# Loading the k of units 4 to 8 with tokens on rows, maxima through memory, and reading channel weights in pairs

## The chip, the cores and the metric

The kernel runs on one core of a Trainium2 chip. The metric is the device time of one execution in microseconds (us); a kernel's time is the median of its runs. Five engines work side by side, each through its own instructions in order: TensorE (PE in the profile, its weight loads PEld), VectorE (DVE), ScalarE (ACT), GpSimd (POOL) and SyncE (SP). Here nearly all loads are issued by SP, so its queue is an order too: a load that has to wait for a buffer holds up every load behind it.

## The reference

Eight batches of eight heads, 576 tokens, head width 64. An attention without a token-by-token matrix is followed by a mixer over tokens and a mixer over channels:

```python
q_s = np.exp(q - np.max(q, axis=-1, keepdims=True))      # softmax of q over the head's 64 columns
q_s = q_s / (np.sum(q_s, axis=-1, keepdims=True) + 1e-09)
k_s = np.exp(k - np.max(k, axis=2, keepdims=True))       # softmax of k over the 576 tokens
k_s = k_s / (np.sum(k_s, axis=2, keepdims=True) + 1e-09)
x = einsum(q_s, einsum(k_s, v))                          # 64x64 per head, then (batch, 576, 512)
h = np.maximum(x.T @ w_tok1, 0.0) @ w_tok2               # tokens: 576 -> 256 -> 576
u = x + h.T
h2 = np.maximum(u @ w_ch1, 0.0) @ w_ch2                  # channels: 512 -> 1536 -> 512
out = u + h2
```

The four weight matrices come as float64, the rest as float32.

## The kernel before

**Units.** A unit is two heads of one batch; there are 32, numbered 0 to 31 here as in the code (n). A unit's tokens lie in five chunks of 128 (the last one is the 64 left-over tokens, laid out twice). Units 0 to 7 (`early`) go through `stage_qT`, `stage_kv`, `stage_y`, `stage_h1` and two `stage_u`: q is turned by TensorE (L349, L354), `kv` is the product of k and v (L319), `y` that of q and w_tok1 (L387), `h1` that of y and kv (L395), and `stage_u` adds q times kv (L440) and the token mixer's second product (`token_products`, L422) into one bank, which `empty` copies to `uh` and `ul`. Units 8 to 31 run later, between the products of the channel mixer.

**The softmax of k** (`softmax_k`) takes its maximum over tokens. Before, units 0 to 7 load only `kt`, the k with the 128 columns on rows: VectorE reduces each row (L249), ScalarE does the exponential (L253), TensorE turns the five chunks back (four at L256, one at L259), and ScalarE copies them out to `k_t` (L257, L260). Unit 8 loads `kt` and `k`: its maxima are spread onto a diagonal, multiplied with ones (L272) and copied to the tile `mb`; GpSimd then subtracts `mb` from `k_t` (L278) and ScalarE does the exponential (L279). Units 9 to 31 do the same, but the maxima get to `mb` through memory: VectorE transposes them in `dg` (L265), SP writes them to `row` in DRAM (L267) and reads that back to all 128 rows (L268). There is one `dg` and one `mb`.

**Weights.** Channel weights come in 24 pieces of 128x512 float64: for each f from 0 to 11 one of w_ch1 and one of w_ch2. `load_ch(f)` loads both. `narrow` makes float32 out of a piece in six steps on 128x512 elements, five on VectorE (L201, L203, L204, L206, L208) and one on ScalarE (L202), and `split` cuts it into a high part (ScalarE) and a low part (VectorE, L126). Pieces take turns in the tiles `stg` of two pools.

**Order.** A scheduler that simulates the program's time line sets the order of the instructions on each engine and in SP's queue. So an instruction that is put in somewhere, or a buffer that comes free at another time, moves others around it. `behind(x)` lets instructions be issued only after those in x. Buffers in the early pools are three deep (`NB`), those of `kt` two.

**Channel mixer.** `ch1` (L477) and `ch2` (L637) work on groups of 512 tokens; steps with f 0 to 3 of the first two groups come first, while later weights are still being narrowed.

Of the kernel before, what the change touches and what calls it, by code (L numbers as in the profile page):

```python
# [8 lines left out]
F32 = mybir.dt.float32  # L9
# [6 lines left out]
P = 128  # L16
# [4 lines left out]
def attn_mixer_kernel(ctx: ExitStack, tc: tile.TileContext, q, k, kt, v, wt, out, dims):  # L21
# [81 lines left out]
    for i in range(3):  # L103
        slots[i][1] = lay.tile([P, NJ, CW], F32R, name=f"ul{i}")
    mb = lay.tile([P, P], F32, name="mb")
    h2 = [[lay.tile([P, CW], F32R, name=f"h2h{i}"), None] for i in range(2)]
    kv_ring = [kv_tile(lay, 0)]
    for i in range(2):
        h2[i][1] = lay.tile([P, CW], F32R, name=f"h2l{i}")
    cw = {}  # L110

    def ch_rows(f0, f1):
        late = ctx.enter_context(tc.tile_pool(name=f"late{f0}", bufs=1))
        t = late.tile([P, f1 - f0, NJ, 4, P], F32R, name=f"cw{f0}")
# [24 lines left out]

    conv = [(stg, cv)]  # L140


    def load_unit(b, j):
        n = b * NJ + j
        u = {"b": b, "j": j, "n": n, "early": n < NE}
        if n >= PAIRED:
            return u
        pool = early if u["early"] else ld
        t = pool.tile([P, C1 * P], F32, name="kt_t", bufs=NB - 1 if u["early"] else 1)
        nc.sync.dma_start(t, kt[n])  # L150
        u["kt"] = t
        t = pool.tile([P, C1, P], F32, name="q_t")
        nc.sync.dma_start(t.rearrange("p c d -> p (c d)"), q[n])
        u["q"] = t
        t = pool.tile([P, C1, P], F32, name="k_t")
        if not u["early"]:
            nc.sync.dma_start(t.rearrange("p c d -> p (c d)"), k[n])
        u["k"] = t
        return u
# [35 lines left out]

    def narrow(raw, n, out):


        w0, w1 = raw[:, 0:n, 0], raw[:, 0:n, 1]
        s = conv[-1][1].tile([P, C1 * P], U32, name="cv_s")[:, 0:n]  # L200
        nc.vector.tensor_scalar(s, w1, 20, 0x7FF, op0=ALU.logical_shift_right, op1=ALU.bitwise_and)  # L201
        nc.scalar.activation(s, s, AF.Relu, bias=ebias, scale=2.0**23)  # L202
        nc.vector.scalar_tensor_tensor(s, w1, 0x80000000, s, op0=ALU.bitwise_and, op1=ALU.bitwise_or)  # L203
        nc.vector.tensor_scalar(w1, w1, 0xFFFFF, 0x100000, op0=ALU.bitwise_and, op1=ALU.bitwise_or)  # L204
        f1 = w1.bitcast(F32)
        nc.vector.scalar_tensor_tensor(f1, w0, 2.0**-32, w1, op0=ALU.mult, op1=ALU.add)  # L206
# [26 lines left out]

    def load_ch(f):
        for x, at in ((0, AT_C1), (2, AT_C2)):
            t = load_weights(at + f).rearrange("p (n m) -> p n m", n=NJ)
            narrowed[:] = [split(cw[f][x], cw[f][x + 1], t, nc.vector)]
# [7 lines left out]
    def softmax_k(u):  # L245
        ktt = u["kt"]
        through = u["n"] > NE
        mc = dg[:, 0:1] if through else sm.tile([P, 1], F32, name="mc")
        nc.vector.tensor_reduce(mc, ktt, axis=AX.X, op=ALU.max)  # L249
        kx = u["k"]  # L250
        if u["early"]:
            nc.vector.tensor_scalar(mc, mc, -1.0, None, op0=ALU.mult)
# [28 lines left out]
    def softmax_q(u):  # L281
# [18 lines left out]
        nc.vector.reciprocal(st[:, 2, :], st[:, 1, :])  # L300
        nc.vector.tensor_tensor(qt, qt, st[:, 2, :].unsqueeze(2).broadcast_to([P, G, D]), op=ALU.mult)
        if u["early"]:
# [439 lines left out]
    for n in range(NE):  # L742
        if n + 2 < NE:
            begin(n + 2)
            soft(n + 2)
        if n + 1 < NE:
            stages[n + 1][0]()
            stages[n + 1][1]()
        stages[n][2]()
        stages[n][3]()  # L750
        if n >= NE - F_HEAD:
            load_ch(n - (NE - F_HEAD))
        if n == NE - 1:
            with behind(emptied):
                split_tok1()
# [211 lines left out]
```

## Time and profile before

| | |
|---|---|
| median of 3 runs | 796.18 us (795.25 to 796.74) |
| the profiled execution | 796.4 us, of which its span is 794.5 us |
| mean granted TensorE clock over the span | 0.994 |
| PE busy | 779.0 us |
| DVE, ACT, POOL busy | 526.7, 326.5, 85.1 us |
| HBM read, written | 54.85 MB, 9.45 MB |

The span is what the profiler saw between the first and the last instruction; the rest of the execution's time lies around it. The shares of the page are means over stages with different limits: units 0 to 7 fill roughly the first 80 us, where VectorE and ScalarE are nearly as busy as TensorE; later TensorE works alone most of the time.

### The profile page before, as it was taken

To read this page: it belongs to the slowest core of one execution; us is meant where nothing else is said; L and a number is where in the kernel's file an instruction comes from. 1 tells how busy PE (TensorE), PEld (TensorE's weight loads), DVE (VectorE), ACT (ScalarE), POOL (GpSimd) and SP (SyncE) were. 2 spreads that over 40 slices of the span, in tenths; PEclk is the share of its full clock that TensorE was granted. 3 is DMA by queue.
4 is the path that set the end of the run, shared out by engine and by line. 5 is a ranking of instruction groups with operands and counts; after the bars stand their busy time and mean duration, and the time that the engine had idled before them with its cause. 6 is when DMAs were issued, how large, how long until landed. Compare 5 with 4: busy or idle time off the path is not lost.

```text
span 794.5 us, 12177 instructions
## 1 busy us (share of the span) xinstructions
PE 779.0 (98%) x4478; PEld 650.9 (82%) x4478; DVE 526.7 (66%) x1208; ACT 326.5 (41%) x824; POOL 85.1 (11%) x77
## 2 busy tenths in 40 slices
PE   6899999999999999999999999999999999999998
PEld 6688888887888888888888888888888888888886
DVE  6899998897777445755575455564668558975441
ACT  6876544435553343344433434333434413232100
POOL 1000010003122111120201101111111000000020
PEclk8899999999999999999999999999999999999999
DMA  9753422334334221513141212313240000000011
GB/s 289 249 175 104 143 91 101 112 89 133 83 92 137 66 72 37 152 37 100 38 120 54 81 57 74 111 38 85 51 125 18 1 1 28 26 1 0 1 67 40
DMA packets 64786, 65.08 MB, mean 82 GB/s; under 512 B 41944, under 2 KB 45272, under 8 KB 64728
## 3 DMA queue, kind: packets, MB, share of 16 engines
q1 hardware_dynamic: 60120, 56.06, 24.1%
q10 hardware_dynamic: 4608, 8.26, 2.8%
q8 instruction: 35, 0.57, 0.3%
q14 instruction: 23, 0.19, 0.1%
HBM read 54.85 MB, written 9.45 MB: 81 GB/s over the span
## 4 chain that ended last, share of the span: by engine, by line
PE 87%; DVE 6%; ACT 3%; DMA 2%; issue 1%; POOL 1%; DVEq 0%; POOLq 0%; ACTq 0%
PE ps_o L637 30%; PE ps_h L477 26%; PE ps_h L586 7%; PE ps_h L387 6%; PE ps_h L422 5%; PE ps_h L637 4%; PE ps_h L319 2%; PE ps_h L456 2%; PE ps_h L395 1%; ACT q_t L292 1%; DMA q_t<-in_q 1%; PE ps_o L422 1%; DVE stack L374 1%; PE ps_o L387 1%; DVE st L286 0%
## 5 line engine op out<-in xcount | busy, mean ns | idle before, releaser
L637 PE MATMUL ps_o<-h2h,cw 128*128 128x512 f32 x768 | 226.6, 391 | 0.0
L477 PE MATMUL ps_h<-uh,cw 128*128 128x512 f32 x672 | 210.4, 393 | 0.0
L637 PEld LDWEIGHTS ps_o<-h2h,cw 128*128 128x128 f32 x768 | 142.5, 188 | 29.8 <-issue 0.4
L481 DVE SCALAR_TENSOR_TENSOR h2l<-ps_h,h2h 128x512 fp32r<-128x512 f32 x84 | 57.8, 688 | 153.2 <-ACT h2h L480 152.6
L477 PEld LDWEIGHTS ps_h<-uh,cw 128*128 128x128 f32 x672 | 123.7, 188 | 24.4 <-issue 0.4
L637 PE MATMUL ps_o<-h2l,cw 128*128 128x512 f32 x384 | 137.4, 390 | 0.0
L477 PE MATMUL ps_h<-ul,cw 128*128 128x512 f32 x336 | 130.9, 390 | 0.0
L480 ACT ACTIVATE h2h<-ps_h 128x512 fp32r<-128x512 f32 x84 | 49.9, 594 | 90.5 <-PE ps_h L477 80.0
L126 POOL TENSOR_TENSOR ql<-q_t,qh 128x640 fp32r<-128x640 f32 x24 | 39.5, 1647 | 425.6 <-ACT qh L125 390.4
L637 PEld LDWEIGHTS ps_o<-h2l,cw 128*128 128x128 f32 x384 | 72.0, 188 | 15.1
L477 PEld LDWEIGHTS ps_h<-ul,cw 128*128 128x128 f32 x336 | 63.1, 188 | 13.4
L374 DVE COPY stack<-cv_s 32x128 f32<-32x128 f32 (+1 forms) x264 | 55.7, 229 | 3.5 <-PE ps_h L456 0.6
L278 POOL TENSOR_TENSOR k_t<-k_t,mb 128x640 f32<-128x640 f32 x24 | 37.9, 1579 | 109.8 <-DMA mb<-row 78.7
L279 ACT ACTIVATE k_t<-k_t 128x640 f32<-128x640 f32 x24 | 17.7, 739 | 66.2 <-POOL k_t L278 66.2
L495 DVE TENSOR_TENSOR ul<-ps_h,ul 128x512 f32<-128x512 f32 x40 | 27.3, 687 | 24.1 <-PE ps_h L586 23.7
L374 ACT COPY stack<-cv_s 32x160 f32<-32x160 f32 (+1 forms) x120 | 37.4, 311 | 2.8 <-DVE cv_s L364 1.5
L434 ACT CAST uh<-ps_h 128x288 fp32r<-128x288 f32 (+8 forms) x84 | 25.1, 317 | 27.2 <-PE ps_h L456 22.6
L297 ACT ACTIVATE q_t<-q_t 128x640 f32<-128x640 f32 x28 | 20.7, 740 | 32.0 <-DVE q_t L296 31.9
L422 PE MATMUL ps_h<-w2h,hh 128*128 128x288 f32 x112 | 33.7, 302 | 0.0
L422 PE MATMUL ps_h<-w2l,hh 128*128 128x288 f32 x112 | 33.3, 298 | 0.0
L637 PE MATMUL ps_h<-cw 128*128 128x512 f32 x144 | 33.0, 389 | 0.0
L422 PE MATMUL ps_h<-w2h,hl 128*128 128x288 f32 x112 | 32.6, 296 | 0.0
(250 smaller groups left out, 1277.0 us busy)
## 6 DMA issues: line engine op xcount, KB each, us to landing
stg<-in_w SPq DMA_DIRECT2D x28, 512.0 KB, 3.3
kt_t<-in_kt SPq DMA_DIRECT2D x32, 320.0 KB, 3.3
q_t<-in_q SPq DMA_DIRECT2D x32, 320.0 KB, 3.0
k_t<-in_k SPq DMA_DIRECT2D x24, 320.0 KB, 3.0
out<-stg ACTq DMA_DIRECT2D x27, 256.0 KB, 2.3
v_t<-in_v SPq DMA_DIRECT2D x46, 128.0 KB, 3.1
part<-in_v SPq DMA_DIRECT2D x18, 128.0 KB
mb<-row SPq DMA_DIRECT2D x23, 64.0 KB, 2.9
```

The lines of the kernel that those rows point to most:

```text
L126: return lo_eng.tensor_tensor(lo, src, f32(hi), op=ALU.subtract).ins
L278: nc.gpsimd.tensor_tensor(kx, kx, mb.unsqueeze(1).broadcast_to([P, C1, P]), op=ALU.subtract)
L374: eng(stack[row : row + Q, h, 0:n, at : at + Q], turned[x * Q : (x + 1) * Q, 0:n, y * Q : (y + 1) * Q])
L387: nc.tensor.matmul(y[:, 0:TOK], a, w, start=(i == 0), stop=(i == len(mm) - 1))
L422: nc.tensor.matmul(t[:, 0:W], a, w, start=start and i == 0, stop=stop and i == len(mm) - 1)
L434: nc.scalar.copy(uh, src).ins,
L477: nc.tensor.matmul(t, cw[f][x][:, n, :], w, start=(i == 0), stop=(i == 3 * NJ - 1))
L480: nc.scalar.activation(hh, t, AF.Relu).ins,
L481: nc.vector.scalar_tensor_tensor(hl, t, 0.0, f32(hh), op0=ALU.max, op1=ALU.subtract).ins,
L495: nc.vector.tensor_tensor(t, a, b, op=op)
L586: nc.tensor.matmul(t, x(n), w[n], start=(n == 0 and i == 0), stop=(n == 1 and i == 2))
L637: nc.tensor.matmul(to, cw[f][x][:, n0 + n, :], w, start=(first and i == 0), stop=(last and i == 2))
```

## The change

Three edits. `NATURAL` is 4: units 4 to 7 now load `k` as well as `kt` and take the way through `row` and `mb` that units 9 to 31 take, and so does unit 8. `exp_k` stands right behind each one's softmax. Their five transposes, ScalarE's two copies and the exponential of `kt` are gone; a load of 320 KB, a small transpose on VectorE, two small transfers, GpSimd's subtraction and the exponential of `k_t` take their place.

While `two` is not empty (f 0 to 7), `load_ch` loads both pieces of an f into one tile of 1024 elements a row and narrows and splits them together, so that a step is one instruction instead of two. f 8 to 11 go as before. The pairs have pools of their own instead of the second `stg` pool.

The loads of a pair are held behind the load of a given unit's q (`loaded`), its first narrowing step behind the end of a given unit's softmax of q (`ready`).

```diff
+    NATURAL = NJ
...
+    nc.gpsimd.memset(dg[:, 0:32], 0.0)
...
-        if not u["early"]:
+        if n >= NATURAL:
             nc.sync.dma_start(t.rearrange("p c d -> p (c d)"), k[n])
...
+    def load_two(at, bt, loaded, begun):
+        pool, place = two[0]
...
+        raw = pool.tile([P, 2 * CW, 2], U32, name="two")
+        with behind(loaded):
+            for x, i in enumerate((at, bt)):
+                nc.sync.dma_start(raw[:, x * CW : (x + 1) * CW, :].rearrange("p n w -> p (n w)"), wt[i].bitcast(U32))
+        return narrow(raw, 2 * CW, None, place.tile([P, 2 * CW], U32, name="two_s"), begun)
...
-    def load_ch(f):
+    def load_ch(f, loaded=(), begun=()):
+        if two:
+            t = load_two(AT_C1 + f, AT_C2 + f, loaded, begun).rearrange("p (x n m) -> p x n m", x=2, n=NJ)
+            hi, lo = (cw_rows[f][:, :, y : y + 3 : 2, :].rearrange("p n x m -> p x n m") for y in range(2))
+            narrowed[:] = [split(hi, lo, t, nc.vector)]
+            return
...
-        through = u["n"] > NE
+        through = u["n"] >= NATURAL
...
-        if u["early"]:
+        if u["n"] < NATURAL:
...
             softmax_k(units[n])
             softmax_q(units[n])
+            if NATURAL <= n <= NE:
+                exp_k(units[n])
...
-            load_ch(n - (NE - F_HEAD))
+
+            f = n - (NE - F_HEAD)
+            load_ch(f, units[min(2 * f + 5, NE - 1)]["loaded"], units[min(f + 5, NE - 1)]["ready"])
...
-    conv[:] = [(stg, cv), (stg_more, cv_more)]
+    conv[:] = [(stg, cv)]
+    two[:] = [[more_pools.enter_context(tc.tile_pool(name=x, bufs=2)) for x in ("two", "two_s")]]
```

Line numbers in the changed kernel are higher by 4 to 31; below, L281 and L284 are the old L256 and L259, L304 the old L279, L317 the old L292.

How the order changes, at three places. First SP's queue around the q of units 3 and 4. In the old program kt_t_547 is unit 4's, q_t_448 and q_t_549 are the q of units 3 and 4, stg_826 and stg_837 the weights of f 0. Before:

```order
L150 DMA kt_t_547<-in_kt 128x640
L180 DMA v_t_136<-in_v 128x4x64 x2
L182 DMA v_t_136<-in_v 32x2x64 x2
L193 DMA stg_826<-in_w 128x1024
L193 DMA stg_837<-in_w 128x1024
L153 DMA q_t_448<-in_q 128x640
L153 DMA q_t_549<-in_q 128x640
L150 DMA kt_t_640<-in_kt 128x640
```

Now, with q_t_455 and q_t_556 for units 3 and 4, kt_t_642 and kt_t_730 for units 5 and 6, and a piece of f 8's weights in stg_1314:

```order
L197 DMA stg_1314<-in_w 128x1024
L184 DMA v_t_143<-in_v 128x4x64 x2
L186 DMA v_t_143<-in_v 32x2x64 x2
L154 DMA kt_t_642<-in_kt 128x640
L292 DMA row_562<-dg_108 4x32
L157 DMA q_t_455<-in_q 128x640
L157 DMA q_t_556<-in_q 128x640
L161 DMA k_t_558<-in_k 128x640
L293 DMA mb_113<-row_562 128x128
L154 DMA kt_t_730<-in_kt 128x640
```

The weights of f 0 have left the place ahead of the two q; kt of unit 5, unit 4's maxima on their way out and one weight piece stand there now, and unit 4's k and `mb` follow.

Second, ScalarE around the ten exponentials of unit 3's q (q_t_448, later q_t_455). Before:

```order
L125 CAST w2h_102<-cv_s_325 128x512
L352 COPY qt_480<-ps_h_481 128x2x256
L355 COPY qt_480<-ps_o_487 128x2x32
L292 ACTIVATE q_t_448,st_464<-q_t_448,st_464 128x64 x10
L389 COPY ys_516<-ps_o_510 128x256
L402 ACTIVATE hh_521<-ps_h_518 128x256
```

Now:

```order
L378 COPY qt_487<-ps_h_488 128x2x256
L381 COPY qt_487<-ps_o_494 128x2x32
L304 ACTIVATE k_t_558<-k_t_558 128x640
L222 ACTIVATE cv_s_343<-cv_s_343,ebias_96 128x128
L317 ACTIVATE q_t_455,st_471<-q_t_455,st_471 128x64 x6
L128 CAST w2h_102<-cv_s_332 128x512
L317 ACTIVATE q_t_455,st_471<-q_t_455,st_471 128x64 x4
L355 ACTIVATE kvf2_149<-ps_h_497,rs_512 64x64 x2
L415 COPY ys_523<-ps_o_517 128x256
L428 ACTIVATE hh_528<-ps_h_525 128x256
```

The exponential of unit 4's k has come ahead of unit 3's q, and the cast of a half of w_tok2 has come in between.

Third, ScalarE ahead of the Relu of unit 2's h1 (hh_614, later hh_616), which TensorE needs for the first product of unit 2 with w_tok2. Before:

```order
L434 CAST uh0_105<-ps_h_535 128x224
L202 ACTIVATE cv_s_839<-cv_s_839,ebias_96 128x512
L402 ACTIVATE hh_614<-ps_o_611 128x256
L389 COPY ys_609<-ps_h_603 128x256
L257 COPY k_t_644<-ps_h_649 128x512
```

Now, with unit 6's k in k_t_734 and the pair of f 0 in two_s_821:

```order
L222 ACTIVATE two_s_821<-two_s_821,ebias_96 128x1024
L460 CAST uh0_105<-ps_h_542 128x224
L304 ACTIVATE k_t_734<-k_t_734 128x640
L460 CAST uh1_106<-ps_o_441 128x64
L428 ACTIVATE hh_616<-ps_o_613 128x256
```

The exponential of unit 6's k stands ahead of that Relu now.

More of the change, by code (lines that the diff above doesn't have):

```diff
@@ L109, in attn_mixer_kernel @@
         h2[i][1] = lay.tile([P, CW], F32R, name=f"h2l{i}")
-    cw = {}
+    cw, cw_rows = {}, {}
     def ch_rows(f0, f1):
@@ L115, in ch_rows @@
         for f in range(f0, f1):
+            cw_rows[f] = t[:, f - f0]
             cw[f] = [t[:, f - f0, :, x, :] for x in range(4)]
@@ L140, in attn_mixer_kernel @@
     conv = [(stg, cv)]
+    two = []
     def load_unit(b, j):
@@ L152, in load_unit @@
         t = pool.tile([P, C1, P], F32, name="q_t")
-        nc.sync.dma_start(t.rearrange("p c d -> p (c d)"), q[n])
+        u["loaded"] = [nc.sync.dma_start(t.rearrange("p c d -> p (c d)"), q[n]).ins]
         u["q"] = t
         t = pool.tile([P, C1, P], F32, name="k_t")
-        if not u["early"]:
+        if n >= NATURAL:
             nc.sync.dma_start(t.rearrange("p c d -> p (c d)"), k[n])
@@ L194, in load_weights, with narrow @@
         return narrow(raw, n, out)
-    def narrow(raw, n, out):
+    def load_two(at, bt, loaded, begun):
+        pool, place = two[0]
+        if not wide:
+            t = place.tile([P, 2 * CW], F32, name="two_s")
+            for x, i in enumerate((at, bt)):
+                nc.sync.dma_start(t[:, x * CW : (x + 1) * CW], wt[i])
+            return t
+        raw = pool.tile([P, 2 * CW, 2], U32, name="two")
+        with behind(loaded):
+            for x, i in enumerate((at, bt)):
+                nc.sync.dma_start(raw[:, x * CW : (x + 1) * CW, :].rearrange("p n w -> p (n w)"), wt[i].bitcast(U32))
+        return narrow(raw, 2 * CW, None, place.tile([P, 2 * CW], U32, name="two_s"), begun)
+    def narrow(raw, n, out, s=None, begun=()):
         w0, w1 = raw[:, 0:n, 0], raw[:, 0:n, 1]
-        s = conv[-1][1].tile([P, C1 * P], U32, name="cv_s")[:, 0:n]
-        nc.vector.tensor_scalar(s, w1, 20, 0x7FF, op0=ALU.logical_shift_right, op1=ALU.bitwise_and)
+        if s is None:
+            s = conv[-1][1].tile([P, C1 * P], U32, name="cv_s")[:, 0:n]
+        with behind(begun):
+            nc.vector.tensor_scalar(s, w1, 20, 0x7FF, op0=ALU.logical_shift_right, op1=ALU.bitwise_and)
         nc.scalar.activation(s, s, AF.Relu, bias=ebias, scale=2.0**23)
@@ L300, in softmax_q @@
         nc.vector.reciprocal(st[:, 2, :], st[:, 1, :])
-        nc.vector.tensor_tensor(qt, qt, st[:, 2, :].unsqueeze(2).broadcast_to([P, G, D]), op=ALU.mult)
+        ready = nc.vector.tensor_tensor(qt, qt, st[:, 2, :].unsqueeze(2).broadcast_to([P, G, D]), op=ALU.mult).ins
+        u["ready"] = [ready]
         if u["early"]:
@@ L711, in attn_mixer_kernel @@
     stg_more = early_pools.enter_context(tc.tile_pool(name="stg_more", bufs=2))
+    two_pools = [early_pools.enter_context(tc.tile_pool(name=x, bufs=2)) for x in ("two", "two_s")]
     conv[:] = [(stg, cv), (stg_more, cv)]
+    two[:] = [two_pools]
     w1f = early1.tile([P, C1, TOK], F32, name="w1f")
@@ L761, in attn_mixer_kernel @@
     more_pools = ExitStack()
-    stg_more = more_pools.enter_context(tc.tile_pool(name="stg_more", bufs=2))
-    cv_more = more_pools.enter_context(tc.tile_pool(name="cv_more", bufs=2))
-    conv[:] = [(stg, cv), (stg_more, cv_more)]
+    conv[:] = [(stg, cv)]
+    two[:] = [[more_pools.enter_context(tc.tile_pool(name=x, bufs=2)) for x in ("two", "two_s")]]
     unit_banks[0] = (ph,)
@@ L845, in attn_mixer_kernel @@
                 more_pools.close()
-                conv[:] = [(stg, cv)]
+                two.clear()
                 ch_rows(F_MORE, NF)
```

## The prediction

> **What bounds the kernel now.** I read the page's first part, then the busy times by stretch, then TensorE's and ScalarE's timelines where TensorE stops waiting, and last SP's issues and GpSimd's instructions.
>
> ```profile
> PE 779.0 (98%) x4478; PEld 650.9 (82%) x4478; DVE 526.7 (66%) x1208; ACT 326.5 (41%) x824; POOL 85.1 (11%) x77
> ...
> 20.00:40.00 20.00, 16.38 (x116) 13.31 (x115) 17.81 (x46) 18.01 (x68) 0.00 (x0) 0.88 0.78 250
> 40.00:60.00 20.00, 19.32 (x165) 17.00 (x164) 19.59 (x50) 15.44 (x42) 0.00 (x0) 1.00 0.60 173
> 60.00:80.00 20.00, 20.00 (x152) 17.66 (x151) 18.66 (x47) 13.16 (x36) 0.00 (x0) 1.00 0.34 101
> ```
>
> A stretch's columns are its length, the busy time of PE, PEld, DVE, ACT and POOL, the granted clock, the DMA share and GB/s. TensorE is idle for 15.5 us of 794.5 in all. From 40 us on it is dense, so there an instruction taken from it shortens the run by its place in the row, and a new wait lengthens it by its length. Before 40 us TensorE waits, mainly for ScalarE and VectorE. The border is seen in TensorE's timeline (start, length, idle before and its releaser):
>
> ```profile
> 30.12 0.71 PE L395 MATMUL ps_o<-kvf,ys 128*128 128x128 f32 x4 [2.06 <-ACT ys L389]
> ...
> 39.54 0.66 PE L349 MATMUL ps_o<-ident,q_t 128*128 128x128 f32 x4
> ...
> 41.56 0.40 PE L422 MATMUL ps_o<-w2h,hh 128*128 128x288 f32 x1 [0.60 <-ACT w2h L125]
> ...
> 42.17 0.80 PE L319 MATMUL ps_o<-v_t,k_t 128*64 128x65 f32 x20
> ```
>
> The row at 39.54 turns unit 3's q; its start is set by ScalarE's exponentials of that q. The wait of 0.60 is the last before the dense part; at 42.17 comes unit 3's kv.
>
> **What is taken from TensorE.** From the chain of waits (start, length, what), where neighbours follow without a gap:
>
> ```profile
> 43.83 0.66 PE ps_h L422 x5
> 44.49 0.44 PE ps_o L395 x4
> 44.93 2.16 PE ps_h L387 x10
> 47.09 0.48 PE ps_h L440 x2
> 47.58 0.44 PE ps_h L256 x4
> ...
> 49.46 0.73 PE ps_h L319 x20
> ...
> 146.15 0.22 PE ps_h L272 x2
> ```
>
> Four transposes of one unit take 0.44 us, so 0.11 each and 0.55 for five. Units 5, 6 and 7 have theirs after 42 us: 3 x 0.55 = 1.65. Unit 4 has its fifth (0.11) behind the row at 39.54; its first four lie ahead of it, where TensorE is early anyway, and I cost them at nothing: what hides them is ScalarE's work on unit 3's q. Unit 8's product with ones is 0.22. Sum: 1.98 us less. The wait of 0.60 goes too, for the cast of w_tok2's tail no longer arrives after TensorE if TensorE is later at the row before it: 2.58 us at most.
>
> **The pairs.** VectorE's steps on 256 and 512 elements:
>
> ```profile
> 20.20 0.43 DVE L203 SCALAR_TENSOR_TENSOR cv_s<-stg,cv_s 128x256 uint32<-128x256 uint32 x1
> ...
> 27.80 0.69 DVE L203 SCALAR_TENSOR_TENSOR cv_s<-stg,cv_s 128x512 uint32<-128x512 uint32 x1
> ```
>
> 256 elements more cost 0.26, so 0.17 of a step does not grow with its size; joining two saves that at most, and less where a step starts before the one ahead of it has ended. Six steps, eight f: 8.2 us of VectorE at most, I take half; all of it off TensorE's path, which waits for no weights from 42 us on. It is a reserve, not a term. Holding f 0's narrowing behind unit 5's softmax moves twelve such steps (up to 8 us of VectorE) back past 50 us; the pairs' saving lies against it. I cost that at nothing; if that cover is gone, TensorE waits for weights (the last rival).
>
> **The new way of k, first place: unit 3's q.** ScalarE's new order puts unit 4's exponential of k and a Relu of 128 elements ahead of unit 3's ten exponentials, and a cast of w_tok2 between them. Everything behind it on ScalarE (unit 3's q, kvf of unit 2, y and hh of unit 1) waits along, and TensorE waits for q and hh. Before:
>
> ```profile
> 30.70 0.42 ACT L202 ACTIVATE cv_s<-cv_s,ebias 128x128 uint32<-128x128 uint32 x1
> ...
> 31.62 0.62 ACT L125 CAST w2h<-cv_s 128x512 fp32r<-128x512 f32 x1
> 32.18 0.59 ACT L352 COPY qt<-ps_h 128x512 f32<-128x512 f32 x1
> ...
> 34.75 0.35 ACT L292 ACTIVATE q_t<-q_t,st 128x64 f32<-128x64 f32 x1 [1.86 <-DVE st L289]
> ```
>
> So ScalarE has 1.86 us to spare there. When does unit 4's k come? Its row maxima and the times of the steps behind them:
>
> ```profile
> 25.71 0.81 DVE L249 TENSOR_REDUCE mc<-kt_t 128x1 f32<-128x640 f32 x1
> ...
> L265 DVE STREAM_TRANSPOSE dg<-dg x23: 167/201/211, 170.7 to 598.3; 128x32 f32<-128x32 f32 x23
> ...
> L267 SPq DMA_DIRECT2D row<-dg x23: 503/508/617, 170.9 to 598.6; - x23
> L268 SPq DMA_DIRECT2D mb<-row x23: 321/329/333, 172.8 to 600.7; - x23
> ...
> DMA to landing us min/median/max: 2.8/2.9/3.3
> ...
> 115.22 3.00 POOL L126 TENSOR_TENSOR ql<-q_t,qh 128x640 fp32r<-128x640 f32 x1 [111.79 <-ACT qh L125]
> 147.62 1.86 POOL L278 TENSOR_TENSOR k_t<-k_t,mb 128x640 f32<-128x640 f32 x1 [29.40 <-ACT mb L273]
> ...
> L278 POOL TENSOR_TENSOR k_t<-k_t,mb x4: 1570/1578/1861, 147.6 to 207.4; 128x640 f32<-128x640 f32 x4
> ...
> L279 ACT ACTIVATE k_t<-k_t 128x640 f32<-128x640 f32 x24 | 17.7, 739 | 66.2 <-POOL k_t L278 66.2
> ```
>
> Maximum at 25.71, 0.8; a step of 0.6 stands between it and the transpose (0.2): 27.3. From the issue of `row` to that of `mb` 1.9 (172.8 less 170.9), then 2.9 to land: 32.1 on a quiet queue. The queue is not quiet:
>
> ```profile
> 25.03 1.08 SPq L193 DMA_DIRECT2D stg<-in_w  x2
> 27.22 0.80 SPq L153 DMA_DIRECT2D q_t<-in_q  x2
> ...
> 33.81 0.82 DVE L286 TENSOR_REDUCE st<-q_t 128x10 f32<-128x640 f32 x1 [0.28 <-DMA q_t<-in_q]
> ```
>
> Behind 1 MB of weights the q issued at 27.22 took over 6 us. Now 512 KB stand there, so I take 32.5, nearer to the quiet value. GpSimd's subtraction is 1.57 at best and 3.00 at worst; with VectorE full as here, 2.0, near the row at 147.62. Then 0.74 for the exponential and 0.3 for the Relu: unit 3's q starts at 35.5 instead of 34.75, plus 0.52 for the cast. TensorE's row at 39.54 moves to 40.8: **+1.27**. Low end: ScalarE is free in time and q lands sooner; TensorE, without unit 4's four transposes, can be there 0.44 earlier: -0.44. High end: 6 us to land and 3.00 on GpSimd: 35.3 + 3.0 + 1.04 = 39.3, so +4.6 + 0.52 = +5.1.
>
> Here the Trainium skill's page "SBUF — State Buffer", section "SBUF: two separate sides", has a rule that speaks against the change: a GpSimd instruction and a VectorE one that reads two SBUF inputs or runs in a 2-port mode exclude each other for the whole instruction. The rows agree: 3.00 instead of 1.57 at 115.22, in VectorE's densest stretch, and the next fence. By that rule the subtraction waits for one VectorE step and takes 2.2 to 2.4; the sum would be 0.2 to 0.4 us higher.
>
> **Second place: unit 2's Relu.** Unit 6's k can only be loaded when unit 3's kv has been computed, as `k_t` has three buffers, and SP has four loads of v ahead of it that wait for the same product. ScalarE's exponential of that k now stands ahead of unit 2's Relu.
>
> ```profile
> 50.10 0.94 SPq L180 DMA_DIRECT2D v_t<-in_v  x2
> 51.14 0.93 SPq L182 DMA_DIRECT2D v_t<-in_v  x2
> ...
> k_t<-in_k SPq DMA_DIRECT2D x24, 320.0 KB, 3.0
> ...
> 68.65 0.38 ACT L402 ACTIVATE hh<-ps_h 128x256 fp32r<-128x256 f32 x1 [1.00 <-PE ps_h L395]
> ```
>
> From the end of unit 3's kv: 2.0 for the four loads of v, 3.0 for k, 2.0 GpSimd, 0.74, and 0.4 for a small cast and the Relu: 8.1 us. TensorE meanwhile has 16 L422 at 0.132 (2.1), 2.16, 0.44, two halves of 0.48, five transposes (0.55) and unit 4's kv (0.73): 7.0. So **+1.1**; low 0 (the loads of v overlap, the queue is quieter), high 2.1 with 3.00 on GpSimd. Units 5 and 7 have over 5 us of slack between landing and kv by the same count; unit 8's k is wanted after 160 us. These I cost at nothing.
>
> **Sum.** -1.98 - 0.60 + 1.27 + 1.1 = -0.2 us on the profiled execution's 796.40: 796.2. That execution lies 0.2 above the median of the runs, 796.18, so the forecast for the median is 796.0. The three runs spread over 1.5 us; I take 0.2%, 1.6 us, as what a measurement tells from no change.
>
> **The rivals.** *The cover holds*: ScalarE's spare 1.86 us and TensorE's 7.0 us hide both ways of k. For it: 512 KB less of weights ahead of that q, and ScalarE loses an exponential and two copies a unit. Against: unit 4's arrival needs every step at its best row. -2.58 and 0.2: 793.4 to 793.6.
>
> *Unit 4's k is late and the clock falls.* Place: ScalarE's queue ahead of unit 3's q. TensorE's gap of 2.06 us at 30.12 was followed by half the clock:
>
> ```profile
> 28.00:30.00 2.00, 0.06 (x1) 0.00 (x0) 2.00 (x5) 1.94 (x6) 0.00 (x0) 1.00 0.97 389
> ...
> 32.00:34.00 2.00, 2.00 (x24) 1.59 (x23) 1.54 (x4) 0.88 (x3) 0.00 (x0) 0.50 0.74 225
> ```
>
> My +1.27 with the 0.44 of removed transposes makes a gap of 1.7. From 2.06 on, a late landing by 1 and 0.4 more on GpSimd (+2.7 in all), the clock may halve over some 3.4 us of dense work: 1.7 us, in which the second place's wait hides. -2.58 + 2.7 + 1.7 = +1.8: 797.8 to 798.5. The Trainium skill's "TensorE: Matmul & The Clock Gate", Part 1, has the clock fall after an idle window of about 3.4 us; by that a gap of 2.1 would not do it and this rival would end at +1.2 with the second wait, yet the rows above show 0.50 after a gap of 2.06, so I keep it.
>
> *VectorE becomes the bound.* GpSimd's five subtractions hold it up:
>
> ```profile
> 148.57 1.47 DVE L206 SCALAR_TENSOR_TENSOR stg<-stg 128x512 f32<-128x512 uint32 x1
> ```
>
> 1.47 where this step takes 0.68: 0.8 lost each, 4.0 in all, against some 2 saved by the first four pairs and 1.75 of idle VectorE between 40 and 80. It decides where the loss passes that; at two steps held per subtraction it costs another 2: 798.2.
>
> **Chances.** Forecast, both waits in part: 0.46, its own range 794.6 to 797.6. Cover holds: 0.27. Late k with the clock: 0.20. VectorE: 0.07. So faster by over 0.2% 0.27, within 0.46, slower 0.27. The range leaves out about a tenth on either side: 793.4 to 798.8, from the first rival to past the second.
>
> **What would show it.** Right: no L256 after 40 us; ScalarE's first exponential of unit 3's q between 34.5 and 37, released by GpSimd's k_t; a wait of TensorE for hh near 50; then dense to 165. Wrong: TensorE dense from 41 us with nothing of GpSimd in its waits (faster), a clock of 0.5 after 40 us, or TensorE waiting for cw between 80 and 160 (slower).

## The result, and the profile after

The changed kernel takes 800.64 us (median) against 795.88 us of the kernel before beside it: a ratio of 1.0064, with a 95% interval of 1.0048 to 1.008. It is slower by 0.6%, 4.8 us; the prediction said 796.0 with a range of 793.4 to 798.8. The profiled execution took 800.12 us with a span of 798.3, 3.8 longer than before. Three executions took far longer than all others (1296.69 us of the kernel before here, 1105.36 of e4 and 1563.25 of e9 below); they stand in the medians, but not in the ratios.

The page's busy times, and the same three stretches as before (length; busy PE, PEld, DVE, ACT, POOL; granted clock, DMA share, GB/s):

```profile
PE 781.0 (98%) x4456; PEld 650.9 (82%) x4456; DVE 528.7 (66%) x1161; ACT 321.8 (40%) x798; POOL 91.7 (11%) x82
...
20.00:40.00 20.00, 13.80 (x103) 10.68 (x102) 17.17 (x43) 15.19 (x56) 1.57 (x1) 1.00 0.73 205
40.00:60.00 20.00, 17.41 (x121) 14.82 (x122) 17.44 (x38) 13.13 (x38) 3.47 (x3) 0.83 0.61 178
60.00:80.00 20.00, 20.00 (x159) 16.71 (x156) 20.00 (x37) 13.25 (x31) 1.16 (x1) 1.00 0.58 190
```

The totals hide what happened: TensorE, ScalarE and VectorE are nearly as busy as before. VectorE lost 47 instructions without getting less to do: added up over the run, the joined steps take 51.1 us where the single ones took 58.0, but the 36 small steps on 128x10 take 11.2 where they took 5.9, since some are held beside GpSimd. The stretches show more. Between 20 and 40 us TensorE works 13.80 us where it was 16.38, between 40 and 60 17.41 where it was 19.32, and the clock there falls to 0.83.

TensorE's row of unit 3's q, with the waits around it (start, length, idle before and its releaser), and the wait at the second place:

```profile
39.94 0.44 PE L448 MATMUL ps_h<-w2h,hh 128*128 128x288 f32 x1 [3.04 <-ACT w2h L128]
...
42.48 0.61 PE L448 MATMUL ps_o<-w2h,hh 128*128 128x288 f32 x1 [0.97 <-ACT hh L428]
...
43.64 1.12 PE L375 MATMUL ps_o<-ident,q_t 128*128 128x128 f32 x4 [0.32 <-DVE q_t L326]
...
54.80 0.40 PE L448 MATMUL ps_h<-w2h,hh 128*128 128x288 f32 x1 [1.02 <-ACT hh L428]
```

The row that stood at 39.54 is at 43.64: 4.10 us later, where 1.27 was forecast. The wait of 1.02 is the second place, forecast at 1.1. After the gap of 3.04 us the clock halves (0.52 in the first four microseconds after 40, 0.63 in the next):

```profile
40.00:44.00 4.00, 2.44 (x7) 1.49 (x8) 3.47 (x7) 3.94 (x16) 1.54 (x1) 0.52 0.97 356
44.00:48.00 4.00, 4.00 (x34) 3.50 (x33) 3.99 (x12) 2.36 (x8) 0.00 (x0) 0.63 0.42 132
```

ScalarE, which the forecast followed:

```profile
36.36 0.74 ACT L304 ACTIVATE k_t<-k_t 128x640 f32<-128x640 f32 x1 [4.32 <-POOL k_t L303]
37.01 0.39 ACT L222 ACTIVATE cv_s<-cv_s,ebias 128x128 uint32<-128x128 uint32 x1
37.30 0.33 ACT L317 ACTIVATE q_t<-q_t,st 128x64 f32<-128x64 f32 x1
...
39.29 0.60 ACT L128 CAST w2h<-cv_s 128x512 fp32r<-128x512 f32 x1
```

Unit 3's ten exponentials begin at 37.30 instead of 34.75 (35.5 forecast). The cast of w_tok2's second half, at 31.62 before, is at 39.29; it is what TensorE's 3.04 us wait for. What holds unit 4's k and that cast shows on SP, GpSimd and VectorE:

```profile
26.48 0.61 SPq L292 DMA_DIRECT2D row<-dg  x1
...
30.71 0.33 SPq L293 DMA_DIRECT2D mb<-row  x1
```

```profile
34.76 1.57 POOL L303 TENSOR_TENSOR k_t<-k_t,mb 128x640 f32<-128x640 f32 x1 [31.26 <-DMA mb<-row]
40.91 1.54 POOL L303 TENSOR_TENSOR k_t<-k_t,mb 128x640 f32<-128x640 f32 x1 [4.58 <-DMA mb<-row]
```

```profile
30.53 0.82 DVE L274 TENSOR_REDUCE dg<-kt_t 128x1 f32<-128x640 f32 x1 [1.86 <-DMA kt_t<-in_kt]
...
34.82 1.54 DVE L314 TENSOR_SCALAR st<-st 128x10 f32<-128x10 f32 x1
36.27 0.68 DVE L228 TENSOR_TENSOR cv_s<-stg,cv_s 128x512 f32<-128x512 f32 x1
...
41.26 1.22 DVE L324 TENSOR_SCALAR st<-st 128x10 f32<-128x10 f32 x1 [0.44 <-ACT q_t L317]
```

From the issue of `row` to that of `mb` 4.2 us pass, and 4.1 from there to the subtraction at 34.76, where I took 32.5 for the landing. VectorE first stands 1.86 us for kt of unit 5, and the last narrowing step of w_tok2's second piece (L228) is behind that maximum and behind a small step that lasts 1.54 us, exactly beside GpSimd's first subtraction; the small step at 41.26, of 1.22 us, stands beside its second. In the old kernel the same narrowing step was at 30.20:

```profile
30.20 0.69 DVE L208 TENSOR_TENSOR cv_s<-stg,cv_s 128x512 f32<-128x512 f32 x1
```

So 4.10 is 2.55 for the later exponentials, 0.5 for the cast between them, and 1.05 for the small step at 41.26 that GpSimd's second subtraction holds, behind which q's last division and its turning wait. This is the chain that the trace shows; the experiments below show that another, through VectorE's order, ends nearly as late.

From there on the two traces are compared by the start of unit 8's kv:

```profile
170.99 0.80 PE L345 MATMUL ps_h<-v_t,k_t 128*64 128x65 f32 x20
```

```profile
165.38 0.80 PE L319 MATMUL ps_h<-v_t,k_t 128*64 128x65 f32 x20
```

It is 5.61 later. 4.10 (first place), 1.02 (second), about 1.7 for the half clock from 43.64 to 46.98, less 1.98 of removed products and 0.60 of the old wait make 4.24; the other 1.4 has no wait of its own in the trace: TensorE is busy through it, with products in another order, and its cause stays open. Behind 171 us 1.8 come back: three of the old kernel's waits there (0.7, 0.4 and 0.3) are gone.

### The profile page after: what moved, and what is told of

It reads as the page before. It is cut to its first block, busy times and chain, and to the rows that moved or that the text cites. A ratio compares the mean times of both kernels' runs of the same rounds, so it can differ in the third digit from the quotient of the medians.

```text
span 798.3 us, 12076 instructions
## 1 busy us (share of the span) xinstructions
PE 781.0 (98%) x4456; PEld 650.9 (82%) x4456; DVE 528.7 (66%) x1161; ACT 321.8 (40%) x798; POOL 91.7 (11%) x82
## 4 chain that ended last, share of the span: by engine, by line
PE 94%; DMA 2%; DVE 2%; ACT 1%; issue 0%; SPq 0%; POOL 0%; DVEq 0%; POOLq 0%
PE ps_o L663 33%; PE ps_h L503 29%; PE ps_h L612 7%; PE ps_h L413 6%; PE ps_h L448 6%; PE ps_h L663 4%; PE ps_h L345 2%; PE ps_h L482 2%; PE ps_h L421 2%; DMA kt_t<-in_kt 1%; PE ps_o L448 1%; PE ps_h L755 1%; PE ps_o L413 1%; PE ps_o L345 0%; ACT q_t L317 0%; DMA v_t<-in_v 0%
## 5 line engine op out<-in xcount | busy, mean ns | idle before, releaser
L303 POOL TENSOR_TENSOR k_t<-k_t,mb 128x640 f32<-128x640 f32 x28 | 45.7, 1633 | 183.0 <-DMA mb<-row 116.6
L304 ACT ACTIVATE k_t<-k_t 128x640 f32<-128x640 f32 x28 | 20.7, 739 | 67.3 <-POOL k_t L303 67.1
```

The costliest lines, as they stand in the source:

```text
L303: nc.gpsimd.tensor_tensor(kx, kx, mb.unsqueeze(1).broadcast_to([P, C1, P]), op=ALU.subtract)
```

## The experiments

Each ran five or more times beside the kernel before, but e16, which ran once; "+" is the distance of its median from that kernel's on the same chip (the changed kernel: +4.8). e1 to e4, e9 and e16 got an order of the scheduler's own. In all others the order of every engine is written out as the changed kernel has it, and single rows are moved; of these the diffs show the main ones in the engine's list (e13 to e15, e17 and e18 move some more). The written-out order without any move did not run, so what writing it out costs by itself is not known. Of the versions in a written-out order only e11 has an interval clear of the changed kernel's (1.0048 to 1.008); where a single one is said to gain or lose against the changed kernel below, this is the distance of two medians whose intervals overlap. Each version also left one trace only.

### One unit less, and the first place by dependences

**e1_unit4_turned**

```diff
-    NATURAL = NJ
+    NATURAL = NJ + 1
```

> Only the k of unit 4 goes back to the old way (kt alone, turned by TensorE); units 5 to 8 and the pairs stay. If the loss sits at the first place (unit 4's k ahead of unit 3's q on ScalarE: 4.1 us, and the 1.7 us of half clock behind it), unit 3's q is turned near 39.5 us again and the time is 800.6 - 5.8 + 0.1 (unit 4's fifth transpose) + 0.6 (the wait for w2h's tail) = 795.5, between 794.5 and 797. If the pairs and the moved loads are the cause, 799.5 or more. If it is GpSimd's five subtractions holding up VectorE, a fifth of the loss goes: 799.7.

807.19 us, +10.7, ratio 1.0139 (1.0119 to 1.0159). Unit 3's row is back at 39.88, as expected, but the time tells nothing of unit 4: the scheduler made another order, with waits of TensorE of 2.4, 2.1 and 1.4 us (at 65.66, 195.67 and 145.41) that neither kernel has.

**e3_exp_behind_q** and **e4_sub_behind_q**: unit 4's exponential, or GpSimd's subtraction, held behind unit 3's q.

```diff
+        with behind(units[3]["exps"] if u["n"] == 4 else []):
             nc.scalar.activation(kx, kx, AF.Exp)
```

> As changed, but ScalarE's exponential of unit 4's k is issued behind the ten exponentials of unit 3's q; GpSimd's subtraction stays where it was. ScalarE's order as the cause: unit 3's exponentials no longer wait for k, but VectorE's small step on unit 3's maxima (34.82, 1.54 us in the changed kernel's trace, beside the subtraction) still releases them near 36.4 instead of 37.3. TensorE's wait of 3.0 us shrinks to 2.1 or less: 800.6 - 0.9 = 799.7 if the clock falls all the same, 797.5 if it doesn't. GpSimd's lock as the cause: 799.7 or more. Pairs: 800.6.

```diff
+        first = [nc.gpsimd.tensor_copy(late, units[3]["q"][:, 0, 0:1]).ins] if u["n"] == 4 else []
+        with behind(first):
             nc.gpsimd.tensor_tensor(kx, kx, mb.unsqueeze(1).broadcast_to([P, C1, P]), op=ALU.subtract)
```

> As changed, but GpSimd's subtraction of unit 4 starts only when VectorE is done with unit 3's q (a copy of one column of that q on GpSimd stands ahead of it), and ScalarE's exponential follows that. This order also puts unit 2's Relu ahead of unit 6's exponential. Lateness of unit 4's k, with or without the lock, as the cause: unit 3's q is turned near 39.5 us again, both waits for hh and the half clock are gone: 800.6 - 4.1 - 1.7 - 1.0 + 0.6 = 794.4, between 793.5 and 796. Unit 4's kv, some 8 us behind, still finds its k. Pairs and moved loads as the cause: 799 or more.

801.61 (1.0063, 1.0047 to 1.008) and 802.41 (1.0069, 1.0055 to 1.0082). In the first, the exponentials of unit 3's q start at 35.28 and its row is at 41.27, 2.4 earlier than in the changed kernel, yet the run is not faster: waits of 1.4 and 1.3 us for w_tok2's two parts come in. In the second, nothing of unit 4's k stands ahead of unit 3's q (the subtraction is at 41.59), and the row is at 42.22 all the same, behind waits of 1.6 and 1.0 us for the same two parts. One added dependence moves rows all over the program. From here the order was fixed.

### Each half alone

**e2_pairs_alone**

```diff
-    NATURAL = NJ
+    NATURAL = NE
```

> The pairs as changed, but only unit 8 (and 9 to 31 as ever) takes the way through memory; units 4 to 7 are turned by TensorE as before. First place or GpSimd's lock as the cause: the loss is gone with the units' k, 795.6 to 796.4, near the old kernel's 795.9. Pairs and moved loads as the cause: 799 to 801.

797.67, +1.1, ratio 1.0017 (1.0008 to 1.0026). TensorE's waits (total, times, longest):

```profile
PE ps_o L448 <- DVE hl L429: 1.3, 1, 1.3
...
PE ps_o L284 <- ACT kvf L355: 1.2, 1, 1.2
```

They are at 82.10 and 48.40; the old kernel has neither. Unit 3's row is at 38.26, so the pairs alone don't delay the first place. The pairs, costed at nothing, cost a microsecond in the order that the scheduler made for them.

**e9_k_alone** and, for its profile, **e16_k_alone_again**: the old kernel with the new way of k and without pairs.

```diff
+    NATURAL = NJ
...
+            if NATURAL <= n <= NE:
+                exp_k(units[n])
```

> The old kernel with the k of units 4 to 8 through memory and nothing else: no pairs, the old pools for weights. The scheduler's own order here has units 1's and 2's Relu and unit 3's ten exponentials ahead of the exponentials of k. Lateness at the two places as the cause: neither is left, TensorE keeps its 1.98 us, GpSimd's lock costs up to 1.5: 794 to 795.5. The new way itself as the cause (GpSimd's lock, one row, one mb, wherever its steps stand): 797 to 799.

> The kernel with the new way of k alone once more, for its profile. It took 798.3 where lateness at two places had 794 to 795.5, so a wait of another kind must stand in TensorE's row: GpSimd's lock on VectorE, or VectorE waiting for the one row or the one dg (seen in the changed kernel's order as 1.78 us ahead of a transpose of dg). The first shows VectorE's steps of 1.2 us and more beside the subtractions, the second VectorE idle for the row's transfer.

798.32, +2.0, ratio 1.0023 (1.0012 to 1.0034); the single execution of e16 took 795.85. No gain either, where 794 to 795.5 was expected. e16's VectorE beside GpSimd's first subtraction, and the product behind it:

```profile
36.38 1.55 POOL L280 TENSOR_TENSOR k_t<-k_t,mb 128x640 f32<-128x640 f32 x1 [32.90 <-ACT q_t L294]
```

```profile
36.63 1.99 DVE L298 TENSOR_TENSOR q_t<-q_t,st 128x640 f32<-128x640 f32 x1
38.54 0.41 DVE L405 SCALAR_TENSOR_TENSOR hl<-ps_h,hh 128x256 fp32r<-128x256 f32 x1
```

```profile
39.01 0.40 PE L424 MATMUL ps_o<-w2h,hl 128*128 128x288 f32 x1 [1.79 <-DVE hl L405]
```

A step of 0.81 took 1.99, hl (the low part of hh, which TensorE multiplies too) came behind it, and TensorE waited 1.79. So GpSimd's hold on VectorE does reach TensorE. But this execution was as fast as the old kernel (795.96 beside it), so its trace doesn't show where the 2.0 of e9 went. The halves sum to 3.1 of 4.8: each costs, and together they seem to cost more, though each half ran in an order of its own.

### One suspected cost at a time, in the changed kernel's order

**e5_exp4_later**, **e8_exp6_later** and both, **e10_exp4_exp6_later**: unit 4's exponential moved behind unit 1's Relu, unit 6's behind unit 2's.

```diff
 ScalarE
-L304 k_t of unit 4
 L317 q_t of unit 3 x10
 ...
 L428 hh of unit 1
+L304 k_t of unit 4
```

> The changed kernel with its order written out as edges, so that every engine keeps it, and one move: ScalarE's exponential of unit 4's k stands behind unit 1's Relu instead of ahead of unit 3's ten exponentials. If the lateness at the two places is the cause, unit 3's exponentials are then released by VectorE's small step beside GpSimd's subtraction (34.82, 1.54 us) and start near 36.4 instead of 37.3: 0.9 us, 799.7; 798.0 if the half clock behind the gap goes too. If the loss is spread over the new order and not at these places, 800.6, as the changed kernel.

```diff
 ScalarE
-L304 k_t of unit 6
 L460 uh
 L428 hh of unit 2
+L304 k_t of unit 6
```

> The changed kernel in its own order with one move: ScalarE's exponential of unit 6's k stands behind unit 2's Relu instead of ahead of it. The second place costs what TensorE waits there, 1.02 us in the trace, with nothing behind it to take it up: 799.6. If another wait takes its place (VectorE's half of that Relu, or the exponential now late for unit 6's kv), 800.6.

> The changed kernel in its own order with both moves: unit 4's exponential of k behind unit 1's Relu, unit 6's behind unit 2's. The two places add up: 800.6 - 1.6 - 1.0 = 798.0. If the second place sets the end of both, so that the first was worth more than it showed alone, 797.4 or less; if one hides the other, 799.

799.02 (+3.2; 1.0038, 1.0025 to 1.005), 799.66 (+3.9; 1.0051, 1.0037 to 1.0066) and 799.91 (+3.6; 1.0042, 1.003 to 1.0054). Singly the medians are 1.5 and 0.9 lower, together 1.2: not a sum, and none of it clear of noise. In e8's trace the wait at the second place is gone, as it should be; but there `mb` also came 1.6 earlier than in the changed kernel's (subtraction at 33.19), so the 0.9 can't be put down to that place. In the first, ScalarE no longer waits for GpSimd, but for VectorE, which GpSimd holds:

```profile
34.47 1.32 DVE L221 TENSOR_SCALAR cv_s<-stg 128x128 uint32<-128x128 uint32 x1
35.71 0.16 DVE L314 TENSOR_SCALAR st<-st 128x10 f32<-128x10 f32 x1
```

```profile
35.88 0.41 ACT L222 ACTIVATE cv_s<-cv_s,ebias 128x128 uint32<-128x128 uint32 x1 [3.19 <-DVE st L314]
36.19 0.33 ACT L317 ACTIVATE q_t<-q_t,st 128x64 f32<-128x64 f32 x1
```

The maxima of unit 3's q are negated at 35.71, in the old kernel's place 34.55. The exponentials start at 36.19, and 1.4 of the 2.55 stay without any k ahead of them.

**e6_subs_one_column** and **e11_and_one_column**: the subtraction of units 4 and 5 works on one column, so that it holds VectorE for next to nothing (the rest of that k stays unsubtracted); in e11 that of units 4 to 7, with both moves above.

```diff
-        nc.gpsimd.tensor_tensor(kx, kx, mb.unsqueeze(1).broadcast_to([P, C1, P]), op=ALU.subtract)
+        m = mb.unsqueeze(1).broadcast_to([P, C1, P])
+        x = (slice(None), slice(0, 1), slice(0, 1)) if u["n"] in (NJ, NJ + 1) else (slice(None),) * 3
+        nc.gpsimd.tensor_tensor(kx[x], kx[x], m[x], op=ALU.subtract)
```

> The changed kernel in its own order, but GpSimd subtracts the maxima of units 4 and 5 from one column of k alone (the other 639 columns keep their maxima), so that it neither takes 1.57 us nor holds VectorE up. Lateness as the cause: ScalarE's exponential of unit 4's k starts 1.5 us earlier, unit 3's exponentials near 35.9 instead of 37.3, and VectorE's step behind them (41.26, 1.22 us, held by the second subtraction) loses 1.1: unit 3's q is turned near 41.1 instead of 43.6, 2.5 us, 798.1; 796.4 if the half clock goes too. If GpSimd's lock doesn't matter and k simply lands late, 1.5 us at most: 799.1. Loss spread over the order: 800.6.

> As the run with both moves, and GpSimd subtracts the maxima of units 4 to 7 from one column of k alone (the other 639 keep theirs), so that VectorE isn't held. With order, lateness and lock all gone unit 3's exponentials start near 34.8 us, its q is turned near 40.3 instead of 43.6, no gap halves the clock in dense work: 800.6 - 3.3 - 1.0 - 1.0 = 795.3, between 794.3 and 796.5. Loss from elsewhere (pairs, seams between products): 797.5 or more.

799.43 (+3.6; 1.0052, 1.0038 to 1.0066) and 798.75 (+2.4; 1.0026, 1.0014 to 1.0038). The medians put GpSimd's hold at about one microsecond here, within the noise. Even with all subtractions and both exponentials out of the way half of the loss is left: unit 3's row is still at 41.02, and TensorE waits 1.1 and 0.8 us for w_tok2's low and high part.

**e7_gap_filled** and **e12_exp6_later_gap_filled**: 22 products whose results are not read stand in TensorE's gap ahead of unit 3's q, to keep the clock up; in e12 unit 6's exponential is moved too.

```diff
+            if u["n"] == 0 and half == 0 and i == 3:
+                for _ in range(22):
+                    nc.tensor.matmul(t[:, CW - P : CW], ones, ones, start=False, stop=False)
```

> The changed kernel in its own order, with 22 idle products of 128x128 (2.4 us at 0.11 each) on TensorE in its gap of 3.04 us ahead of the row at 39.94; their results are not read. If the gap is what halves the clock from 40.15 to 46.98, the clock stays at 1.0 there and the dense 3.3 us of that stretch take half: 800.6 - 1.7 = 798.9. If the half clock comes from something else, or is hidden by the waits, 800.6.

> The changed kernel in its own order with unit 6's exponential behind unit 2's Relu, and the 22 idle products in the first gap as well. When the gap alone was filled, TensorE got to unit 2's Relu earlier and waited there for 2.4 us instead of 1.0, so the half clock's price was hidden; with that wait gone it shows: 799.7 - 1.7 = 798.0. If the half clock costs nothing: 799.7.

801.28 (+5.5; 1.006, 1.0046 to 1.0074) and 800.97 (+4.6; 1.0046, 1.0029 to 1.0062): no gain. In the first the clock stays whole from 40 to 48 and unit 3's row comes 1.0 earlier, at 42.66. But then TensorE waits longer at the second place, and the clock halves there:

```profile
PE ps_h L451 <- ACT hh L428: 2.4, 1, 2.4
```

```profile
54.00:58.00 4.00, 3.17 (x12) 2.90 (x13) 3.53 (x11) 2.55 (x9) 0.00 (x0) 0.62 0.57 128
```

So the price of the half clock at the first place could not be measured by itself: time won there is waited away at the next place. In e12's profile `mb` landed so late (subtraction at 37.87) that unit 3's row was at 46.50; it decides nothing.

### VectorE's order

**e13_vector_order**, **e15_scalar_order_alone** and **e14_vector_order_exp4_first**. In e13 VectorE narrows w_tok2 first and negates unit 3's maxima at once, and ScalarE has the cast and then the q ahead of unit 4's k (and unit 2's Relu ahead of unit 6's). e15 has e13's ScalarE with the changed kernel's VectorE; e14 is e13 with unit 4's exponential back ahead of unit 3's.

```diff
 VectorE
-L274 dg, maxima of unit 5's k
 L224 L129 L226 L228 w_tok2
 L311 L314 st, maxima of unit 3's q, negated
+L274 dg, maxima of unit 5's k
 ScalarE
+L128 w2h
-L304 k_t of unit 4
 L317 q_t of unit 3 x10
 ...
 L428 hh of unit 1
+L304 k_t of unit 4
```

> The changed kernel, TensorE, GpSimd and SP in its own order; VectorE and ScalarE in another between 28 and 45 us. VectorE: the maximum of unit 5's k, which waits 1.86 us for its load at 28.67, stands behind the narrowing of w_tok2's second piece and unit 3's maxima, and the small step on these (34.82 before) right behind them. ScalarE: the cast of w_tok2 ahead of unit 3's exponentials, those of unit 4's and 6's k behind units 1's and 2's Relu. VectorE's order as the cause of the first place: the exponentials of unit 3's q start near 32.7 instead of 37.3, its q is turned near 37.7 instead of 43.6, and TensorE keeps what was taken from it: 792 to 795. If the loads set the end (v and k behind unit 3's kv), TensorE waits later instead: 796 to 799.

> ScalarE's order as in the two runs before it, VectorE's as in the changed kernel. VectorE's order as the cause: the cast of w_tok2 waits for VectorE until 36.9 and the exponentials behind it start at 37.5, so the first place stays: 799 to 801. ScalarE's order as the cause: as the first of these runs, 795 or less.

> As the run before it, but the exponential of unit 4's k stays ahead of unit 3's exponentials on ScalarE. It prices the late k of unit 4 by itself in an order where nothing else is late: the exponentials of unit 3's q then wait for GpSimd until some 37 us, 4.4 us later than in the run before it, and that run's time plus 3 to 5 follows. If the late k matters little, within 1.5 of it.

801.82 (1.0067, 1.0055 to 1.0079), 800.92 (1.0061, 1.0047 to 1.0074) and 803.29 (1.009, 1.0073 to 1.0106). TensorE's row of unit 3's q in e13, in e15 and in e14, then the wait in e15, and ScalarE in e14:

```profile
38.55 0.66 PE L375 MATMUL ps_o<-ident,q_t 128*128 128x128 f32 x4
```

```profile
42.57 1.12 PE L375 MATMUL ps_o<-ident,q_t 128*128 128x128 f32 x4
```

```profile
42.01 1.05 PE L375 MATMUL ps_o<-ident,q_t 128*128 128x128 f32 x4
```

```profile
PE ps_h L448 <- DVE w2l L129: 3.7, 1, 3.7
```

```profile
35.78 0.74 ACT L304 ACTIVATE k_t<-k_t 128x640 f32<-128x640 f32 x1 [3.50 <-POOL k_t L303]
36.43 0.33 ACT L317 ACTIVATE q_t<-q_t,st 128x64 f32<-128x64 f32 x1
```

With both orders repaired the row is at 38.55, a microsecond ahead of the old kernel's. With ScalarE's alone (e15) it stays at 42.57, with a wait of 3.7. With VectorE's alone (e14) it stays at 42.01: ScalarE stands 3.50 us for unit 4's k, and unit 3's exponentials begin at 36.43 instead of 32.53 in e13. So two hold-ups stand side by side at the first place, unit 4's late k and VectorE's order, and either is enough to keep the row late. e14 is e13 with unit 4's exponential ahead of unit 3's; this moves the row by 3.46, and the median of the run by 1.5.

But e13 is not faster. The five microseconds won at 38 are lost by 58: in a wait of 0.94 at 46.38, one of 2.54 at 51.18, and the clock at half from there. ScalarE, then TensorE, around the second:

```profile
49.35 1.15 ACT L222 ACTIVATE two_s<-two_s,ebias 128x1024 uint32<-128x1024 uint32 x1 [2.07 <-DVE two_s L221]
...
50.73 0.40 ACT L428 ACTIVATE hh<-ps_o 128x256 fp32r<-128x256 f32 x1
```

```profile
51.18 0.61 PE L448 MATMUL ps_h<-w2h,hh 128*128 128x288 f32 x1 [2.54 <-ACT hh L428]
```

The first pair's step on ScalarE waits 2.07 for VectorE and lasts 1.15, and unit 2's Relu stands behind it.

**e17_both_places_in_order** moves that step behind the Relu (and VectorE's pair steps likewise); **e18_third_place_too** goes on to the place that then appears.

```diff
 ScalarE (e17)
-L222 two_s
 L428 hh of unit 2
+L222 two_s
 SP (e18)
-L293 mb of unit 7
 L184 L186 v_t
 L161 k_t
 L157 q_t
+L293 mb of unit 7
```

> The run with VectorE's order put right turned unit 3's q at 38.55, 5.1 us ahead of the changed kernel, and TensorE then waited 0.94 and 2.54 at 46 to 51 us: ScalarE stood 2.07 us for VectorE's first step on a pair and worked 1.15 us on that pair's 1024 elements, both ahead of unit 2's Relu, and the clock was halved from 51.10 to 57.93. Here that order goes on to 55 us: the pair's steps on ScalarE and VectorE, the maxima of unit 6's q (which wait for their load) and the exponentials of units 5's and 6's k stand behind units 2's and 3's Relu, and unit 3's kv is normalised as soon as it is there. If waits made by the order are the whole cause, TensorE is dense from 38.5 us on and the time is 799.7 (that profile) - 3.4 - 3.4 = 793, between 792 and 795.5, less than the old kernel. If each wait taken away is given back at the next load (k of unit 6, q of unit 6), 797 or more.

> The run before it kept TensorE dense from 39.54 to 64 us but for one wait of 1.17, and gave it back there: SP's queue stood from 49.8 to 54.05 us for the one mb (until GpSimd was done with unit 6's), with the loads of v, of unit 7's k and of its q behind it; so unit 7's k was late, its exponential stood 5.32 us in ScalarE's queue ahead of a copy of q, TensorE waited 3.10 at 64.24 and the clock was halved from 64.80 to 71.63. Here SP issues unit 7's mb behind those loads, ScalarE does that exponential behind unit 4's Relu, and w_tok2's low part and the copies of unit 4's q stand earlier (waits of 1.27 and 1.17). If the order is the cause all along, 801.3 - 3.1 - 3.4 - 1.2 - 1.0 = 792.6, between 791.5 and 795. If each repair is given back later, 797 or more.

801.3 (1.0066, 1.0052 to 1.008) and 800.34 (1.0051, 1.0037 to 1.0065): both missed by far. In e17 SP's queue stands from 49.78 to 54.05 at the load of unit 7's `mb`, of which there is one: GpSimd reads unit 6's from it until 54.02. ScalarE then stands for unit 7's k, and TensorE for ScalarE. GpSimd, SP, ScalarE, TensorE:

```profile
52.16 1.86 POOL L303 TENSOR_TENSOR k_t<-k_t,mb 128x640 f32<-128x640 f32 x1 [9.62 <-DMA k_t<-in_k]
```

```profile
49.41 0.37 SPq L157 DMA_DIRECT2D q_t<-in_q  x1
54.05 0.33 SPq L293 DMA_DIRECT2D mb<-row  x1
```

```profile
61.86 0.74 ACT L304 ACTIVATE k_t<-k_t 128x640 f32<-128x640 f32 x1 [5.32 <-POOL k_t L303]
```

```profile
64.24 0.66 PE L375 MATMUL ps_h<-ident,q_t 128*128 128x128 f32 x4 [3.10 <-ACT qt L381]
```

In e18 all three are gone, unit 3's row is at 38.33, and TensorE waits again, three times between 60 and 80 us, for VectorE and ScalarE:

```profile
60.76 0.66 PE L375 MATMUL ps_h<-ident,q_t 128*128 128x128 f32 x4 [1.59 <-DVE ul L461]
...
79.94 0.40 PE L448 MATMUL ps_h<-w2h,hl 128*128 128x288 f32 x1 [1.55 <-DVE hl L429]
```

```profile
60.00:80.00 20.00, 16.53 (x117) 13.16 (x117) 19.48 (x37) 12.18 (x29) 1.74 (x1) 1.00 0.46 144
```

VectorE is busy 19.48 of 20 us there, in steps of a pair's length. In the changed kernel it is busy 20.00 of the same 20 us and TensorE waits for nothing, so a full VectorE alone doesn't make TensorE wait. Whether another order of VectorE would keep what the repairs win, or the work of 60 to 80 us is simply too much for it, stays open. No version that ran beats the old kernel.

## Why the prediction was wrong, step by step

- **What is taken from TensorE: right.** The last transposes of k are at 30.6, unit 8's product with ones is gone, and so is the old wait of 0.60.
- **The first place: the mechanism stood at the right place, and the term was mis-sized**, 4.10 for 1.27, inside the bounds given for it (-0.44 to +5.1). Unit 4's k came 2.3 later than I took (34.76 for 32.5), because I took the landing nearer to the quiet queue's value than to the 6 us of the q beside it; GpSimd's own time was 1.57, better than the 2.0 taken. The small step at 41.26 that GpSimd's second subtraction holds, 1.05, was not in the sum at all. Neither was a second hold-up, as I followed ScalarE's order only: VectorE's order, in which unit 5's maximum stands ahead of w_tok2's narrowing, ends that narrowing 6.1 us later (36.27 for 30.20), and TensorE waits for its cast. e14 and e15 show that the late k and VectorE's order each keep the row late alone (42.01 and 42.57), e13 that it is early without both (38.55).
- **The half clock behind the first place: put at nothing in the sum.** It takes about 1.7 by the trace. I had it in a rival only, where the gap was to be longer than in the forecast.
- **The pairs and the narrowing moved back, "costed at nothing": wrong.** e2 measures +1.1 for the pairs alone, in its own order. Which step makes e2's two waits was not followed; e13 shows one way in which a pair can cost: a step of 1.15 us on ScalarE that waits for VectorE stands ahead of a Relu. Fewer instructions are also longer ones, and what stands behind such a step waits for all of it.
- **The second place: right**, 1.02 for 1.1. By the trace TensorE had 7.6 us of work from unit 3's kv on where 7.0 was taken, and the way to the Relu took 8.6 where 8.1 was; the two errors cancel, so that the size is this close is in part luck. With unit 6's exponential moved (e8) the wait is gone.
- **"From 40 us on it is dense, so an instruction taken shortens the run": the premise fell.** It holds while the feeding engines are ahead by more than is won. e7, e13, e17 and e18 each turn unit 3's q 1.0 to 5.3 us earlier than the changed kernel and wait it away by 80 us.
- **GpSimd against VectorE.** By the rule of the Trainium skill, "SBUF — State Buffer", section "SBUF: two separate sides", a GpSimd instruction and a VectorE one that reads two SBUF inputs or runs in a 2-port mode exclude each other, and the one that starts first keeps the port pair for its whole instruction. By it I made the subtraction 2.2 to 2.4 long, with GpSimd as the one that waits. In the changed kernel it was first, at 34.76 and 40.91, and took 1.57 and 1.54, and VectorE's steps begun at 34.82 and 41.26 took the delay (in which mode these ran no trace shows). In e5 it was second, at 40.64, and took 2.22. Both agree with first come, first served.
- **The rivals.** Late k with the clock is the nearest: its gap, its half clock and the second wait are in the profile, and its 797.8 to 798.5 lacks two more microseconds. VectorE as the bound had 0.07; its hold beside GpSimd is seen (1.54 and 1.22 in the changed kernel, 1.99 in e16), but how much of the end it makes is not shown. That the cover holds is refuted by the waits at both places. Of the signs named ahead, a wait for hh came near 55 us, and of those for being wrong the clock of 0.5 after 40 us. The clock gate of the Trainium skill, "TensorE: Matmul & The Clock Gate", Part 1, wants an idle window of about 3.4 us; the clock fell after gaps of 3.04 us here and 2.4 in e7, as after 2.06 in the old kernel, so it was right not to lean on it.

## What to carry to other kernels

When an order is made by a scheduler, follow every in-order queue between the moved instruction and the engine that bounds, not the one the diff touches: here a second hold-up, enough by itself, sat in VectorE's order while the sum was made on ScalarE's. A dense engine is only worth shortening where its feeders have more slack than is won; otherwise repairs carry the wait to the next place, four times in this case. And before pricing one step by an experiment, write out the order and move that step alone, with a run of the written-out order unmoved beside it (which this case lacks), since a small edit can cost more elsewhere than the step is worth (e1: 6 us more than the change itself).

## What the runs showed of the hardware

- GpSimd's subtraction on 128x640 and VectorE's product of q on 128x640 (L326) met in two runs: in e5 VectorE's began first, at 40.61, and took 0.83, and the subtraction, begun at 40.64, took 2.22; in e8 the subtraction began first, at 40.04, and took 1.54, and VectorE's, begun at 40.12, took 2.15. A step on 128x10 with a single input from memory is held too: 1.54 and 1.22 us in the changed kernel where it takes 0.16 in e5.
- The way of one small array through memory takes unlike times in kernels that have the same order up to there: from the issue of `row` for unit 4 to GpSimd's subtraction 8.28 us in the changed kernel, 6.89 in e8 and 9.11 in e12 (one execution each).
- The half clock follows TensorE's gaps: after one of 3.04 us in the changed kernel, 2.54 in e13 and 2.4 in e7, where the earlier gap was filled. Several short ones do it as well: in e10 the longest was 1.36, with one of 0.86 behind it, and the clock was at 0.50 from 40 us; a single one of 1.79 in e16 left it at 1.00.
